# Weights converted with three DVE passes and two ACT passes per pair of pieces, the first block's attention ahead of the conversion, the checks moved behind it

## The chip, the cores and the metric

One core of a Trainium2 chip runs the program. It has five engines with a queue each: PE (TensorE, matrix products), DVE (VectorE), ACT (ScalarE), POOL (GpSimd) and SP (SyncE, which here issues all DMAs). Each queue is worked off in order. [...] The metric is the device time of one execution in microseconds (us).

## The reference

A recurrent attention (RWKV-6) over 4 batches, 8 heads, 768 steps and 48 channels, followed by a two-layer network with a hard-swish between the layers:

```python
for t in range(S):
    kt, vt, rt, wt = (k[:, :, t], v[:, :, t], r[:, :, t], w[:, :, t])
    cur = np.einsum('bhd,bhe->bhde', u[None] * kt, vt)
    y[:, :, t] = np.einsum('bhd,bhde->bhe', rt, state + cur)
    state = wt[:, :, :, None] * state + np.einsum('bhd,bhe->bhde', kt, vt)
...
x = np.ascontiguousarray(attn_out.transpose(0, 2, 1, 3)).reshape(B * S, H * D)
h = x @ w_in
relu6 = np.clip(h + 3.0, 0.0, 6.0)
g = h * relu6 / 6.0
return (g @ w_out).astype(np.float32)
```

x is 3072 x 384, w_in 384 x 2048 and w_out 2048 x 384. [...]

## The kernel before, in words

The 3072 tokens are 24 chunks of 128 (six per batch); three chunks are a block, so there are 8 blocks. For each chunk:

- `load` (L90) issues two DMAs on SP: `feat_in` (r, k, w with the channels on the partitions) and `tok_in` (r, k, v with the tokens there). Three and four buffers.
- `prep` (L138) makes the running product `W` of w (DVE scan, L141), its reciprocal `inv` (DVE, L145), `R` and `K` (POOL, L148 and L149), the tokens' own term `rk` and `dg` (POOL L154 and L155, DVE L157), and spreads `dg` on the diagonal of a tile `A` for all 8 heads (POOL, L160). For the checks it notes the largest w (`w_max`, DVE L150) and the last running product (`w_min`, DVE L152).
- `score` (L165): K times R on PE into `a_ps` (L170), then DVE copies the part above the diagonal into `A` (L173).
- `turn_k` and `write`: PE turns K (L184), ACT copies it (`kn`, L186), PE makes the chunk's state (L195), DVE adds it to `base` (L203, L205), POOL multiplies it with W to the new state `S` (L207).
- `read` (L212): PE adds the part from the state (L223) and the part from `A` (L228); ACT copies the output into `xT` and `x3` (L233, L234). After a block's third chunk six small DMAs on SP move `x3` into `xT` (L239).

For each block the network runs: 16 times `up` (L241: three PE products L246, on ACT `r6` L249, on DVE the gate `g` L251; four PSUM buffers named `mm`), then for each of 3 chunks 4 pieces of `down` (L256: four products L264 each, at the end ACT copies `o`, L268, and SP stores it). A float32 product is two passes on PE, so an `up` is six passes and a whole block of `up` 96, as many as a block of `down`.

The weights come in 32 pieces (16 of w_in, 16 of w_out, 128 x 384 words each) through `weights` (L31): a DMA into `bits` (three buffers, L42), then seven DVE passes (L49 to L58) that take mantissa, exponent and sign apart and put a float32 together. `some_weights` hands out the pieces between the steps of the chunks: 2 before chunk 0, then 3, 2 and 3 in each chunk, so that all are handed out within the first four chunks or so. A list `todo` holds the network's pieces of the finished blocks; each chunk takes a share of it so that PE has work between its own steps.

The code is written in program order; a scheduler and the tile pools decide where an instruction stands on its engine, so the order below is that of the built program. At the end a flag is made of w_max and w_min (L324 to L331). If it were set, `general_path` would compute everything again; with these inputs it is not taken.

Of the kernel before, what the change touches and what calls it, by code (L numbers as in the profile page):

```python
# [18 lines left out]
L = 128  # L19
GP = 64  # L20
LEVELS = 7
BC = 3
LEAST = 2.0 ** -60

# [39 lines left out]
def fast_path(tc, feat, tok, ub, moe_w_in, moe_w_out, out, flag, n_chunks):  # L64
# [15 lines left out]
    with ExitStack() as ctx:  # L80
# [21 lines left out]
        load(1)  # L102

        w_in = const.tile([128, NFC, NCC, 128], F32, name="w_in")
        w_out = const.tile([128, NFC, DM], F32, name="w_out")
        weights = weight_loader(nc, io, wk, w_in, w_out, moe_w_in, moe_w_out)
# [28 lines left out]
        w_max = const.tile([PR, NT], F32, name="w_max")  # L135
        w_min = const.tile([PR, NT, P], F32, name="w_min")

        def prep(i):  # L138
            d = st[i]
            W_ = wk.tile([PR, P * (L + 1)], F32, name="W")  # L140
            nc.vector.tensor_tensor_scan(out=W_, data0=d["w"], data1=restart.rearrange("q p t -> q (p t)"),  # L141
                                         initial=0.0, op0=ALU.mult, op1=ALU.add)
            W = W_.rearrange("q (p t) -> q p t", p=P)
            inv = wk.tile([PR, P, L], F32, name="inv")
            nc.vector.reciprocal(out=inv, in_=W[:, :, 1:])  # L145
# [3 lines left out]
            nc.gpsimd.tensor_mul(K, d["k"], inv)  # L149
            nc.vector.tensor_reduce(out=w_max[:, i:i + 1], in_=d["w"], axis=AX.X, op=ALU.max,  # L150
                                    apply_absolute_value=True)
            nc.vector.tensor_copy(out=w_min[:, i, :], in_=W[:, :, L])  # L152
            rk = wk.tile([L, HD], F32, name="rk")
            nc.gpsimd.tensor_mul(rk, d["rt"], d["kt"])  # L154
            nc.gpsimd.tensor_mul(rk, rk, u_bc)  # L155
            dg = wk.tile([L, H, 1], F32, name="dg")
            nc.vector.tensor_reduce(out=dg.rearrange("s h o -> s (h o)"), in_=rk.rearrange("s (h d) -> s h d", d=D),  # L157
                                    axis=AX.X, op=ALU.add)
            A = wk.tile([L, H, L], F32, name="A")
            nc.gpsimd.tensor_mul(A, ident.rearrange("s (o t) -> s o t", o=1).to_broadcast([L, H, L]),  # L160
                                 dg.to_broadcast([L, H, L]))
            d.update(W=W, R=R, K=K, A=A)
# [79 lines left out]
        def up(bk, f):  # L242
# [7 lines left out]
            g = wk.tile([128, MB], F32, name="g", bufs=NFC + 4)  # L250
# [22 lines left out]
        pieces = [("in", f) for f in range(NFC)] + [("out", f) for f in range(NFC)]  # L273

        def some_weights(n):
            for piece in pieces[:n]:
                weights(*piece)
            del pieces[:n]

        def mlp(n):  # L280
            for _ in range(min(n, len(todo))):
                f, bk, j = todo.pop(0)
                f(bk, j)
# [3 lines left out]
        prep(0)  # L287
        prep(1)
        some_weights(2)
        done = 0  # L290
        for i in range(NT):
            goal = max(0, (i - BC + 1) * per_block // BC - lag) - done
            done += max(goal, 0)
            left = goal
# [7 lines left out]
            if i + 2 < NT:  # L302
                load(i + 2)
            score(i)
            turn_k(i)
            some(1)
            if i + 1 < NT and i > 0:
                prep(i + 1)
            some(2)
            some_weights(3)  # L310
            write(i)
            some(1)
            some_weights(2)
            read(i)
            some(left)
            some_weights(3)
            if i % BC == BC - 1:
                bk = i // BC
                todo.extend([(up, bk, f) for f in range(NFC)] + [(down, bk, c) for c in range(BC * QD)])
                if i == NT - 1:  # L320

                    low = wk.tile([PR, 1], F32, name="low", bufs=1)
                    top = wk.tile([PR, 1], F32, name="top", bufs=1)
                    nc.vector.tensor_reduce(out=low, in_=w_min.rearrange("q i p -> q (i p)"), axis=AX.X, op=ALU.min,  # L324
                                            apply_absolute_value=True)
                    nc.vector.tensor_reduce(out=top, in_=w_max, axis=AX.X, op=ALU.max)
                    nc.vector.tensor_scalar(out=low, in0=low, scalar1=LEAST, scalar2=None, op0=ALU.is_lt)
                    nc.vector.scalar_tensor_tensor(out=top, in0=top, scalar=1.0, in1=low, op0=ALU.is_gt, op1=ALU.max)
                    n_ps = pp.tile([1, 1], F32, name="ps")
                    nc.tensor.matmul(n_ps, lhsT=top, rhs=ones[0:PR, :], start=True, stop=True)  # L330
                    nc.vector.tensor_copy(out=flag, in_=n_ps)  # L331
# [240 lines left out]
def kernel(  # L572
# [3 lines left out]
    tok: bass.AP,  # L576
    ub: bass.AP,
# [19 lines left out]
    fast_path(tc, feat, tok, ub, moe_w_in, moe_w_out, out, flag, n_chunks)  # L597
# [5 lines left out]
_INS = ['feat', 'tok', 'ub', 'ug', 'moe_w_in', 'moe_w_out']  # L603
# [59 lines left out]
```

## Time and profile before

| what | value |
|---|---|
| runs | 720.85, 721.9, 722.49 us, median 721.9 |
| the profiled execution | 722.04 us, span 720.0 us |
| busy in the span | PE 624.5 us (87%), DVE 360.1, POOL 185.7, ACT 128.4 |
| mean granted PE clock | 0.936 of full |
| HBM | 43.49 MB read, 4.72 MB written |

The span goes from the first to the last instruction of the program; the rest of the execution's time lies around it. In the profile a line such as `L49 DVE TENSOR_SCALAR man<-bits ... x32 | 19.4, 606` is a group: line, engine, operation, what it writes from what, shapes, count, then busy us in all and mean ns of one, then the engine's idle time before these and what ended it. PEld is PE's weight load, which runs beside its products.

### The profile page before, as it was taken

The page shows a single profiled execution, that of the slowest core. Times are in us where ns is not written, and L with a number is a line of the kernel's source. Part 1 is how long each engine was busy: PE and PEld are TensorE (multiplying, and loading weights), DVE is VectorE, ACT ScalarE, POOL GpSimd, SP SyncE. Part 2 cuts the span into 40 slices and gives each one's busy share as a digit, 9 for nine tenths or more (in the row PEclk, how much of TensorE's full clock was granted, in tenths as well). Part 3 has the DMA queues.
Part 4 walks back from the last instruction along what each step waited for, and adds up shares of the span by engine and source line. Part 5 has one row for each costly group of instructions (what it writes and reads, how often), then busy time and mean ns, then how long its engine had stood idle before and what let it go on. Part 6 is the DMA issues. An engine that isn't in the chain of part 4 may idle for free.

```text
span 720.0 us, 6998 instructions
## 1 busy us (share of the span) xinstructions
PE 624.5 (87%) x2706; PEld 392.4 (54%) x2706; DVE 360.1 (50%) x548; ACT 128.4 (18%) x269; POOL 185.7 (26%) x148
## 2 busy tenths in 40 slices
PE   1341373779999999999999999999999999999996
PEld 1330251546666666666666666666666666655553
DVE  6999999998136525640346337512463152101200
ACT  0010011112013201320123012210331023102300
POOL 5532252345143223322313413420342020000000
PEclk9975575779999999999999999999999999999999
DMA  8454444423030122211112203120210000000000
GB/s 253 156 166 148 149 148 143 126 72 99 31 93 34 39 90 68 73 64 53 45 50 72 90 16 117 54 71 12 82 34 9 22 12 1 8 24 11 1 12 25
DMA packets 20410, 49.93 MB, mean 69 GB/s; under 512 B 2448, under 2 KB 12560, under 8 KB 20368
## 3 DMA queue, kind: packets, MB, share of 16 engines
q1 hardware_dynamic: 20368, 49.40, 22.2%
q8 instruction: 23, 0.38, 0.2%
q14 instruction: 19, 0.16, 0.1%
HBM read 43.49 MB, written 4.72 MB: 67 GB/s over the span
## 4 chain that ended last, share of the span: by engine, by line
PE 78%; DVE 19%; DMA 2%; POOL 1%; issue 0%; ACT 0%; ACTq 0%; DVEq 0%; POOLq 0%
PE mm L264 35%; PE mm L246 33%; PE a_ps L170 3%; PE ps L228 3%; DVE man L49 2%; DVE inv L145 2%; DVE mag L56 2%; DVE mag L51 2%; PE ps L223 2%; PE ps L195 2%; DVE ex L55 2%; DVE ex L52 1%; DVE W L141 1%; DVE w_out L58 1%; DVE ex L54 1%; PE ps L184 1%
## 5 line engine op out<-in xcount | busy, mean ns | idle before, releaser
L246 PE MATMUL mm<-xT,w_in 128*128 128x384 f32 x768 | 266.9, 504 | 10.4 <-DMA xT<-x 6.6
L264 PE MATMUL mm<-w_out,g 128*128 128x384 f32 x768 | 255.0, 488 | 0.0
L246 PEld LDWEIGHTS mm<-xT,w_in 128*128 128x128 f32 x768 | 148.4, 197 | 110.9 <-issue 16.4
L264 PEld LDWEIGHTS mm<-w_out,g 128*128 128x128 f32 x768 | 143.6, 190 | 96.5 <-issue 2.4
L251 DVE SCALAR_TENSOR_TENSOR g<-r,mm 128x384 f32<-128x384 f32 x128 | 69.5, 550 | 113.0 <-ACT r L249 112.5
L249 ACT ACTIVATE r<-mm,half 128x384 f32<-128x384 f32 x128 | 74.4, 581 | 209.3 <-PE mm L246 178.5
L207 POOL TENSOR_TENSOR S<-base,W 112x448 f32<-112x448 f32 x20 | 19.7, 983 | 254.8 <-DVE base L205 180.1
L145 DVE RECIPROCAL inv<-W 112x512 f32<-112x512 f32 x24 | 80.4, 3349 | 0.6
L160 POOL TENSOR_TENSOR A<-ident,dg 128x1024 f32<-128x1024 f32 x24 | 49.8, 2076 | 41.2 <-PE ps L228 21.2
L170 PE MATMUL a_ps<-R,K 48*128 48x128 f32 x384 | 33.0, 317 | 31.0 <-POOL K L149 31.0
L173 DVE COPY_PREDICATED A<-mask,a_ps 128x1024 f32<-128x1024 uint8 x24 | 31.2, 1301 | 57.0 <-PE a_ps L170 56.9
L170 PEld LDWEIGHTS a_ps<-R,K 48*128 48x128 f32 x384 | 27.7, 216 | 45.2 <-POOL K L149 34.5
L233 ACT COPY xT<-ps 48x384 f32<-48x384 f32 x48 | 22.7, 473 | 155.6 <-PE ps L228 155.2
L148 POOL TENSOR_TENSOR R<-feat_in,W 112x512 f32<-112x512 f32 x24 | 32.3, 1346 | 69.3 <-DVE W L141 66.5
L228 PE MATMUL ps<-A,tok_in 128*48 128x128 f32 x384 | 29.4, 302 | 21.4 <-DVE A L173 21.4
L223 PE MATMUL ps<-R,S 112*112 112x128 f32 x160 | 23.9, 296 | 25.3 <-POOL S L207 25.3
L141 DVE TENSOR_TENSOR_SCAN W<-feat_in,restart 112x516 f32<-112x516 f32 x24 | 34.3, 1430 | 18.9 <-POOL S L207 14.8
L149 POOL TENSOR_TENSOR K<-feat_in,inv 112x512 f32<-112x512 f32 x24 | 30.8, 1282 | 36.3 <-DVE inv L145 13.7
L223 PEld LDWEIGHTS ps<-R,S 112*112 112x112 f32 x160 | 22.3, 195 | 31.1 <-POOL S L207 26.3
L157 DVE TENSOR_REDUCE dg<-rk 128x8 f32<-128x384 f32 x24 | 13.2, 549 | 48.1 <-POOL rk L155 48.1
L228 PEld LDWEIGHTS ps<-A,tok_in 128*48 128x48 f32 x384 | 22.6, 135 | 26.6 <-issue 13.1
L268 ACT COPY o<-mm 128x384 f32<-128x384 f32 x24 | 11.5, 479 | 117.5 <-PE mm L264 108.3
(42 smaller groups left out, 303.2 us busy)
## 6 DMA issues: line engine op xcount, KB each, us to landing
feat_in<-in_feat_dram SPq DMA_DIRECT2D x24, 673.8 KB, 4.9
tok_in<-in_tok_dram SPq DMA_DIRECT2D x24, 576.0 KB, 3.9
bits<-in_moe_w_in_dram SPq DMA_DIRECT2D x16, 384.0 KB, 3.3
bits<-in_moe_w_out_dram SPq DMA_DIRECT2D x16, 384.0 KB, 3.1
out_dram<-o SPq DMA_DIRECT2D x24, 192.0 KB, 1.9
xT<-x SPq DMA_DIRECT2D x48, 24.0 KB, 2.5
u_bc<-in_ub_dram SPq DMA_DIRECT2D x1, 192.0 KB, 7.0
```

The source lines that it names most:

```text
L141: nc.vector.tensor_tensor_scan(out=W_, data0=d["w"], data1=restart.rearrange("q p t -> q (p t)"), initial=0.0, op0=ALU.mult, op1=ALU.add)
L145: nc.vector.reciprocal(out=inv, in_=W[:, :, 1:])
L148: nc.gpsimd.tensor_mul(R, d["r"], W[:, :, :L])
L160: nc.gpsimd.tensor_mul(A, ident.rearrange("s (o t) -> s o t", o=1).to_broadcast([L, H, L]), dg.to_broadcast([L, H, L]))
L170: nc.tensor.matmul(a_ps[:, g, p, :], lhsT=d["K"][rows, p, :], rhs=d["R"][rows, p, :], start=True, stop=True)
L173: nc.vector.copy_predicated(out=d["A"].rearrange("s (p g) t -> s g p t", g=2), mask=mask.rearrange("s (o x t) -> s o x t", o=1, x=1).to_br ...
L223: nc.tensor.matmul(y_ps[:, p, :], lhsT=st[i - 1]["S"][:, p, :], rhs=d["R"][:, p, :], start=(p == 0), stop=False, skip_group_check=True)
L228: nc.tensor.matmul(y_ps[g * GP:g * GP + D, p, :], lhsT=d["v"][:, h, :], rhs=d["A"][:, h, :], start=(first and p == 0), stop=(p == P - 1), ...
L246: nc.tensor.matmul(h_ps, lhsT=w_in[:, f, j, :], rhs=b["xT"][:, j, :], start=(j == 0), stop=(j == NCC - 1))
L249: nc.scalar.activation(out=r6, in_=h_ps, func=ACT.Relu, bias=half, scale=1.0 / 6.0)
L251: nc.vector.scalar_tensor_tensor(out=g, in0=r6, scalar=1.0, in1=h_ps, op0=ALU.min, op1=ALU.mult)
L264: nc.tensor.matmul(o_ps, lhsT=b["g"][f][:, c * L:(c + 1) * L], rhs=w_out[:, f, :], start=(f == 0), stop=(f == NFC - 1))
```

## The change

Six things change in `fast_path`; `general_path` keeps the old conversion.

1. The pieces are converted in 16 pairs (768 words per partition) by `fast_weights`. ACT makes a small integer from each low word in two passes (`more`, L93 and L94), DVE shifts and masks the high word (`top`, L95 and L97) and adds both (L99). This holds for a limited range of exponents.
2. The attention of chunks 0, 1 and 2 stands in the program ahead of all conversion; `load(2)`, `load(3)` and `load(4)` are issued before the first pair's DMAs.
3. The 16 conversions are put in front of the first block's 16 `up` pieces: three pairs before the first, the other 13 spread over the 16.
4. The check of w no longer runs in `prep`: it reads w again from DRAM (`wflat`, 6 pieces of 128 x 1536), and both weight matrices are read again to check the exponents (16 pieces of 128 x 768, two reduces each). Two of these 22 checks follow each chunk from chunk 6 on; they share the buffers of `bits`.
5. The diagonal of `A` is made by ACT, one pass per head (L225), instead of one POOL instruction (L160), and `w_min` is copied by ACT (L216) instead of DVE.
6. `g` has 19 buffers instead of 20.

```diff
+def fast_weights(nc, io, wk, w_in, w_out, moe_w_in, moe_w_out):
...
+        bits = io.tile([128, n], I64, name="bits", bufs=3)
+        for x in range(2):
+            nc.sync.dma_start(out=bits.rearrange("p (c j) -> p c j", j=128)[:, x * m:(x + 1) * m], in_=srcs[x])
...
+        nc.scalar.activation(out=more, in_=lo, func=ACT.Copy, bias=2.0 ** 23, scale=2.0 ** -29)
+        nc.scalar.activation(out=more.bitcast(I32), in_=more, func=ACT.Copy, bias=-2.0 ** 23, scale=1.0)
+        nc.vector.tensor_scalar(out=top, in0=hi, scalar1=3, scalar2=0x3FFFFFF8,
+                                op0=ALU.logical_shift_left, op1=ALU.bitwise_and)
+        nc.vector.scalar_tensor_tensor(out=top, in0=hi, scalar=-0x40000000, in1=top,
+                                       op0=ALU.bitwise_and, op1=ALU.bitwise_or)
+        nc.vector.tensor_tensor(out=dst, in0=top, in1=more.bitcast(I32), op=ALU.add)
...
+        def vet_w(j):
+            t = io.tile([128, VN], F32, name="bits", bufs=3)
+            nc.sync.dma_start(out=t, in_=wflat[:, j * VN:(j + 1) * VN])
+            nc.vector.tensor_reduce(out=w_max[:, j:j + 1], in_=t, axis=AX.X, op=ALU.max, apply_absolute_value=True)
+
+        def vet_weights(which, j):
...
+            nc.sync.dma_start(out=t, in_=src[:, j * n:(j + 1) * n])
+            hi = t.bitcast(F32).rearrange("p (j two) -> p j two", two=2)[:, :, 1]
+            for o, op in ((word_max, ALU.max), (word_min, ALU.min)):
+                nc.vector.tensor_reduce(out=o[:, which, j:j + 1], in_=hi, axis=AX.X, op=op, apply_absolute_value=True)
...
-            nc.vector.tensor_reduce(out=w_max[:, i:i + 1], in_=d["w"], axis=AX.X, op=ALU.max,
-                                    apply_absolute_value=True)
-            nc.vector.tensor_copy(out=w_min[:, i, :], in_=W[:, :, L])
+            nc.scalar.copy(out=w_min[:, i, :], in_=W[:, :, L])
...
-            nc.gpsimd.tensor_mul(A, ident.rearrange("s (o t) -> s o t", o=1).to_broadcast([L, H, L]),
-                                 dg.to_broadcast([L, H, L]))
+            for h in range(H):
+                nc.scalar.activation(out=A[:, h, :], in_=ident, func=ACT.Copy, scale=dg[:, h])
...
+        prep(0)
+        prep(1)
+        attend(0)
+        prep(2)
+        attend(1)
+        attend(2)
+        ahead = 3
+        convs = [(weights, which, f) for which in ("in", "out") for f in range(0, NFC, 2)]
+        first = pieces_of(0)
+        for p in range(NFC):
+
+            upto = ahead + -(-(len(convs) - ahead) * (p + 1) // NFC)
+            before = 0 if p == 0 else ahead + -(-(len(convs) - ahead) * p // NFC)
+            first[p] = convs[before:upto] + first[p]
+        todo.extend(first)
+        load(3)
+        prep(3)
...
+            attend(i, some)
+            if i + 1 < NT:
+                prep(i + 1)
+            some(left)
+            if i >= 2 * BC:
+                for f, *args in vets[:2]:
+                    f(*args)
+                del vets[:2]
```

Here `attend` is `score`, `turn_k`, `write` and `read` of a chunk with shares of `todo` between them.

On DVE, before, right behind the preparation of chunk 1, the first pieces' conversion begins; the predicated copy (L173) of chunk 0 follows it:

```order
L157 TENSOR_REDUCE dg_139<-rk_136 128x8
L49 TENSOR_SCALAR man_145<-bits_143 128x384
L52 TENSOR_SCALAR ex_147<-bits_143 128x384
L51 SCALAR_TENSOR_TENSOR mag_146<-bits_143,man_145 128x384
L54 TENSOR_SCALAR ex_147<-ex_147 128x384
L49 TENSOR_SCALAR man_157<-bits_155 128x384
L55 TENSOR_SCALAR ex_147<-ex_147 128x384
L51 SCALAR_TENSOR_TENSOR mag_158<-bits_155,man_157 128x384
L56 SCALAR_TENSOR_TENSOR mag_146<-mag_146,ex_147 128x384
L52 TENSOR_SCALAR ex_159<-bits_155 128x384
L58 SCALAR_TENSOR_TENSOR w_in_84<-bits_143,mag_146 128x384
```

On DVE, now, the copies L237 of chunks 1 and 2 (A_152, A_216) and their state steps L269 stand ahead of the first pairs (top_368, top_378); `dg_333` to `inv_323` belong to chunk 3:

```order
L237 COPY_PREDICATED A_152<-mask_102,a_ps_225 128x2x4x128
L269 TENSOR_TENSOR base_1_109<-S_185,ps_242 48x4x48 x2
L221 TENSOR_REDUCE dg_333<-rk_330 128x8
L207 SCALAR_TENSOR_TENSOR W_321<-feat_in_317,restart_104 112x516
L211 RECIPROCAL inv_323<-W_321 112x512
L237 COPY_PREDICATED A_216<-mask_102,a_ps_268 128x2x4x128
L269 TENSOR_TENSOR base_0_107<-S_249,ps_285 48x4x48 x2
L95 TENSOR_SCALAR top_368<-bits_365 128x768
L95 TENSOR_SCALAR top_378<-bits_375 128x768
L97 SCALAR_TENSOR_TENSOR top_368<-bits_365,top_368 128x768
L97 SCALAR_TENSOR_TENSOR top_378<-bits_375,top_378 128x768
```

The conversion has moved behind the attention of three chunks and into fewer, longer rows; the adds L99 follow as `ISA w_in_88<-top_368,more_369 128x1536`. A little further, around the first gate (g_411), DVE's order is now:

```order
L207 SCALAR_TENSOR_TENSOR W_495<-feat_in_344,restart_104 112x516
L221 TENSOR_REDUCE dg_507<-rk_504 128x8
L315 SCALAR_TENSOR_TENSOR g_411<-r6_409,mm_405 128x384
L211 RECIPROCAL inv_497<-W_495 112x512
L95 TENSOR_SCALAR top_398<-bits_395 128x768
L95 TENSOR_SCALAR top_416<-bits_413 128x768
```

The gate waits for its `up`, and the reciprocal of chunk 4 and two pairs wait behind it. On SP, before, two pieces of weights go out after the second chunk's loads:

```order
L92 DMA feat_in_80<-in_feat_dram 112x1540
L93 DMA tok_in_81<-in_tok_dram 128x1152
L42 DMA bits_143<-in_moe_w_in_dram 128x3x128
L42 DMA bits_155<-in_moe_w_in_dram 128x3x128
L92 DMA feat_in_167<-in_feat_dram 112x1540
```

On SP, now, the loads of chunks 3 and 4 (feat_in_317 to tok_in_345) stand ahead of the first three pairs, and the six small DMAs of block 0 ahead of the next three:

```order
L132 DMA feat_in_317<-in_feat_dram 112x1540
L133 DMA tok_in_318<-in_tok_dram 128x1152
L132 DMA feat_in_344<-in_feat_dram 112x1540
L133 DMA tok_in_345<-in_tok_dram 128x1152
L86 DMA bits_365<-in_moe_w_in_dram 128x3x128 x2
L86 DMA bits_375<-in_moe_w_in_dram 128x3x128 x2
L86 DMA bits_385<-in_moe_w_in_dram 128x3x128 x2
L132 DMA feat_in_518<-in_feat_dram 112x1540
L303 DMA xT_187<-x3_188 16x384 x6
L86 DMA bits_395<-in_moe_w_in_dram 128x3x128 x2
```

The fifth token buffer in a row (tok_in_345) is the first one's again, so that load waits until chunk 0's output is done, and the first pairs wait behind it.

More of the change, by code (lines that the diff above doesn't have):

```diff
@@ L300, in some @@
                 left -= n
[L302 to L307, printed above, removed]
-                prep(i + 1)
[L309 to L314, printed above, removed]
+            if i + 1 < NT:
+                load(i + 1)
+            attend(i, some)
+            if i + 1 < NT:
+                prep(i + 1)
@@ L315, in fast_path @@
             some(left)
-            some_weights(3)
+            if i >= 2 * BC:
+                for f, *args in vets[:2]:
+                    f(*args)
+                del vets[:2]
             if i % BC == BC - 1:
[L318 to L331, printed above, removed]
@@ L332, in fast_path @@
+        n_ps = pp.tile([1, 1], F32, name="ps")
+        nc.tensor.matmul(n_ps, lhsT=bad, rhs=ones, start=True, stop=True)
+        nc.vector.tensor_copy(out=flag, in_=n_ps)
         mlp(len(todo))
@@ L600 @@
         general_path(tc, feat, tok, ug, moe_w_in, moe_w_out, out, n_chunks)
-_INS = ['feat', 'tok', 'ub', 'ug', 'moe_w_in', 'moe_w_out']
+_INS = ['feat', 'tok', 'wflat', 'ub', 'ug', 'moe_w_in', 'moe_w_out']
 _OUTS = [((3072, 384), 'float32')]
```

88 lines of the change are left out of this document (69 added, 19 removed).

## The prediction

> **What bounds the kernel now.** I read the page's slices first, then the chain that ended last, then the stretch table cut where the chain changes hands.
>
> ```profile
> span 720.0 us, 6998 instructions
> PE   1341373779999999999999999999999999999996
> DVE  6999999998136525640346337512463152101200
> PEclk9975575779999999999999999999999999999999
> PE 78%; DVE 19%; DMA 2%; POOL 1%; issue 0%; ACT 0%; ACTq 0%; DVEq 0%; POOLq 0%
> ```
>
> From the second to the ninth slice (18 us each) DVE is full and PE mostly not, at a lowered granted clock; from the tenth on PE is full. The chain in order of time gives the first pair of passes of a `down` (L264) and the last ones:
>
> ```profile
> 172.34 2.58 PE mm L264 x8
> ...
> 683.54 30.97 PE mm L264 x96
> ```
>
> The last pass ends at 683.54 + 30.97 = 714.51. Cutting there:
>
> ```profile
> 86.97:172.34 85.37, 59.13 (x217) 36.37 (x218) 84.28 (x159) 12.33 (x25) 36.87 (x23) 0.73 0.36 112
> 172.34:714.51 542.17, 542.16 (x2343) 336.62 (x2341) 196.13 (x250) 108.87 (x227) 116.11 (x95) 1.00 0.15 45
> ```
>
> The columns are length, then busy time (count) of PE, PEld, DVE, ACT, POOL, then clock, DMA share and GB/s. After 172.34 PE has 0.01 us of idle time in 542.17, at clock 1.00: that stretch gets shorter only if PE has less to do. From the first `up` (86.97) to the first `down` DVE is busy 84.28 of 85.37 us. So the question of the change is one number: when does the first `down` start?
>
> **What the conversion costs DVE.** By line, shapes apart:
>
> ```profile
> L49 DVE TENSOR_SCALAR man<-bits 128x384 int32<-128x384 int32 x32 | 19.4, 606 | 1.1 <-DMA bits<-in_moe_w_in_dram 1.1
> L51 DVE SCALAR_TENSOR_TENSOR mag<-bits,man 128x384 f32<-128x384 uint32 x32 | 19.1, 597 | 0.0
> L56 DVE SCALAR_TENSOR_TENSOR mag<-mag,ex 128x384 f32<-128x384 f32 x32 | 18.5, 579 | 0.1
> L55 DVE TENSOR_SCALAR ex<-ex 128x384 int32<-128x384 int32 x32 | 14.2, 443 | 0.1
> L52 DVE TENSOR_SCALAR ex<-bits 128x384 int32<-128x384 int32 x32 | 12.8, 398 | 0.0
> L54 DVE TENSOR_SCALAR ex<-ex 128x384 int32<-128x384 int32 x32 | 11.0, 345 | 0.0
> L58 DVE SCALAR_TENSOR_TENSOR w_out<-bits,mag 128x384 int32<-128x384 int32 x16 | 10.9, 679 | 0.0
> L58 DVE SCALAR_TENSOR_TENSOR w_in<-bits,mag 128x384 int32<-128x384 int32 x16 | 9.5, 597 | 0.0
> ```
>
> Together 115.4 us. Undisturbed, one follows the other faster than it lasts:
>
> ```profile
> 29.03 0.35 DVE L52 TENSOR_SCALAR ex<-bits 128x384 int32<-128x384 int32 x1
> 29.30 0.55 DVE L58 SCALAR_TENSOR_TENSOR w_in<-bits,mag 128x384 int32<-128x384 int32 x1
> 29.77 0.35 DVE L54 TENSOR_SCALAR ex<-ex 128x384 int32<-128x384 int32 x1
> ```
>
> From start to start a one-input pass takes 0.27 us and a two-input pass 0.47, so a piece takes 4 x 0.27 + 3 x 0.47 = 2.49 us and a pair 4.98. The durations undisturbed would sum to 32 x (4 x 0.35 + 3 x 0.55) = 97.6; the other 17.8 us are passes held up while POOL works, as here:
>
> ```profile
> 21.85 3.97 DVE L49 TENSOR_SCALAR man<-bits 128x384 int32<-128x384 int32 x1
> 22.75 1.90 POOL L160 TENSOR_TENSOR A<-ident,dg 128x1024 f32<-128x1024 f32 x1
> ```
>
> After, a pair of 768 words is one one-input pass, one two-input pass and the add. Doubling the pitches (an upper bound, since the fixed part is doubled too): 0.54 + 0.94 = 1.48 us. The add (L99) stands in the order as `ISA` on 128x1536, that is on halves of words, and no such instruction is in the trace. Its ends: 0.94 as a two-input pass of 768 words, or 1.88 at one half word in the time of a word. I take 0.94, since L58 writes the same words to the same tile. That makes 2.42 us a pair. [...]
>
> **The start, until the first `up`.** Chunks 0 to 2 now run with no conversion between them. Their chain is read off the trace of before:
>
> ```profile
> 14.72 2.08 PE L170 MATMUL a_ps<-R,K 48*128 48x128 f32 x16 [14.72 <-POOL K L149]
> ...
> 33.34 2.08 PE L170 MATMUL a_ps<-R,K 48*128 48x128 f32 x16
> ...
> 40.57 1.11 PE L228 MATMUL ps<-A,tok_in 128*48 128x128 f32 x16
> ...
> 86.97 1.62 PE L246 MATMUL mm<-xT,w_in 128*128 128x384 f32 x2 [6.64 <-DMA xT<-x]
> ```
>
> ```profile
> 81.41 0.26 ACT L234 COPY x<-ps 48x128 f32<-48x128 f32 x1
> ```
>
> ```profile
> L249 ACT ACTIVATE r<-mm,half 128x384 f32<-128x384 f32 x128 | 74.4, 581 | 209.3 <-PE mm L246 178.5 <-DVE g L251 30.8
> ```
>
> The first scores start at 14.72, and nothing ahead of them gets shorter but small DVE passes. Chunk 1 took 41.68 - 33.34 = 8.34 us from scores to output. Three of those end at 39.7. The diagonal tiles come now from ACT, ahead of `kn` in its queue: eight passes of 128 elements, each between 0.26 (L234, as many elements, no operand per partition) and 0.58 (L249, three times as many, with one), nearer the first; so 2.1 to 4.6 a chunk. Between 0 (hidden behind DVE's reciprocal) and 14 us in all, I take 3. From the last copy to the first `up` went 86.97 - 81.41 = 5.6 us, mostly six small DMAs in line. First `up`: 39.7 + 3 + 5.6 = 48.3. The first three pairs are converted before that: their DMAs stand behind a `tok` load that waits for chunk 0's output (14.72 + 8.34 + 3, about 26), and they have until about 43 to land.
>
> **From the first `up` to the first `down`.** Besides 13 pairs, DVE has 16 gates, 2 reciprocals, a scan, 2 predicated copies and a reduce here:
>
> ```profile
> L145 DVE RECIPROCAL inv<-W 112x512 f32<-112x512 f32 x24 | 80.4, 3349 | 0.6
> L251 DVE SCALAR_TENSOR_TENSOR g<-r,mm 128x384 f32<-128x384 f32 x128 | 69.5, 550 | 113.0 <-ACT r L249 112.5
> L160 POOL TENSOR_TENSOR A<-ident,dg 128x1024 f32<-128x1024 f32 x24 | 49.8, 2076 | 41.2 <-PE ps L228 21.2 <-DVE dg L157 20.1
> L141 DVE TENSOR_TENSOR_SCAN W<-feat_in,restart 112x516 f32<-112x516 f32 x24 | 34.3, 1430 | 18.9 <-POOL S L207 14.8 <-DMA feat_in<-in_feat_dram 3.9
> L173 DVE COPY_PREDICATED A<-mask,a_ps 128x1024 f32<-128x1024 uint8 x24 | 31.2, 1301 | 57.0 <-PE a_ps L170 56.9
> L150 DVE TENSOR_REDUCE w_max<-feat_in 112x1 f32<-112x516 f32 x24 | 16.3, 680 | 18.8 <-DMA feat_in<-in_feat_dram 18.8
> L152 DVE COPY w_min<-W 112x4 f32<-112x4 f32 x24 | 9.5, 395 | 0.0
> L157 DVE TENSOR_REDUCE dg<-rk 128x8 f32<-128x384 f32 x24 | 13.2, 549 | 48.1 <-POOL rk L155 48.1
> ```
>
> 13 x 2.42 + 16 x 0.55 + 2 x 3.35 + 1.43 + 2 x 1.30 + 0.55 = 51.5 us. Three additions. The first gate stands in DVE's order ahead of a reciprocal and conversions and so makes them wait: its `up` is six passes, at the half clock of the row at 86.97 6 x 0.81 = 4.9 us, at full clock 6 x 30.97/96 = 1.9, plus 0.58 for ACT: between 2.5 and 5.5, I take 5. Hold-ups by POOL: between 39 x 17.8/224 = 3 (by instruction) and 17.8 x 13/16 = 14.5 (by pair); POOL loses L160 (2.08 us a chunk), so I take 5. Less 1 for the last add, which no gate waits for. First `down`: 48.3 + 51.5 + 5 + 5 - 1 = 108.8, call it 108.
>
> ACT has 26 conversion passes there, each under 2 x 0.581 = 1.16 us, 30 in all, 16 r6 (9.3) and 16 diagonal passes (4 to 9): at most 49 of 60 us, hidden behind DVE as long as the data is there. DMA:
>
> ```profile
> bits<-in_moe_w_in_dram SPq DMA_DIRECT2D x16, 384.0 KB, 3.3
> feat_in<-in_feat_dram SPq DMA_DIRECT2D x24, 673.8 KB, 4.9
> 54.00:72.00 18.00, 2.31 (x11) 1.72 (x9) 16.92 (x42) 0.53 (x1) 4.33 (x3) 0.50 0.50 148
> SPq L93 <- PE ps L228: 185.0, 18, 18.0
> ```
>
> 13 pairs of 768 KB and about three chunks' loads are 14 MB in 60 us, 233 GB/s; the row had 148 at half the engines' share, so 296 at full share: 47 us, hidden with 13 to spare. SP's token loads wait for PE as before; the bits behind them wait too, but three pairs are in hand.
>
> **After the first `down`** PE's list is the one of before but for eight state passes that move ahead (at most 8 x 0.32 = 2.6 us less, put at zero), so 542.17 us remain. DVE's load there: 196.1, less 18 x (0.68 + 0.40) = 19 for the two steps that leave DVE (L150, L152), plus the checks: 6 reduces of 1536 elements and 32 of 768, from L150's 516 about 2.0 and 1.0 us, 44: about 221 of 542. ACT gains about 45 on 108.9, POOL loses 37. A gate behind a late check may slip: `mm` has four buffers and an `up` takes 1.9 us, so PE feels only more than about 5.8. I put zero on the path. One `g` buffer less costs nothing: the fourth next gate reuses a tile whose last `down` is long past.
>
> **Sum.** 720.0 - (172.34 - 108) = 655.7 us of span. The profiled execution took 722.04 in all, 2.04 outside the span, and the median of the runs is 721.9, so: 658 us.
>
> **The rivals.**
> - *The add runs at one half word a step:* 13 x 0.94 = 12 us more, 670. For it: the 1536 in the order. Against: the bytes are those of 768 words. 0.09.
> - *No cost for ACT's diagonals, full clock and no hold-ups:* 108 - 3 - 2.5 - 5 = 97.5, 647. For it: POOL's work falls. 0.07.
> - *PE's clock, not the conversion, sets the start,* so that the change does not do what it says: 96 `up` passes at half clock are 62 us and three chunks 25, the first `down` at 48 + 87 = 135, 685. For it: clock 0.50 in the row from 54. Against: 0.73 between 86.97 and 172.34, although PE waited for DVE. [...] 0.08.
> - *DMA sets the pace:* if 148 GB/s is all that such loads give, 14 MB take 95 us, first `down` at 143, 693. Decides below 233 GB/s. Against: the share of 0.50. 0.06.
> - *Slower than before: the checks stop PE.* 22 checks stand in DVE's line ahead of gates, their DMAs in SP's line behind loads and outputs that wait. If each held PE for its landing and reduces (3.3 + 2.0), that is 117 us, less the 64 gained: +53, 775. It decides at 64/22 = 2.9 us of idle PE per check. Against: four `mm` buffers, and DVE under half busy. 0.03.
>
> **How the numbers follow.** The forecast (first `down` at 99 to 117) gets 0.67. With 670 and 647 the range 644 to 676 holds 0.83. Faster 0.96, within 0.2% (1.4 us, about what can be told here) 0.01, slower 0.03, all of it the checks.
>
> **What would show it.** Right: a first `up` near 48, the first `down` near 108, then about 542 us of PE without gaps; the add near 0.94; DVE full between the two. Wrong: DVE idle there with waits on bits or on r6, clock 0.5 through it, or idle PE time later that ends on gates behind the checks.

## The result, and the profile after

| | before | after |
|---|---|---|
| median of 4 runs | 722.19 us (720.85 to 722.49) | 648.43 us (647.21 to 649.35) |
| profiled execution | 722.04, span 720.0 | 649.35, span 647.6 |
| first `up` | 86.97 | 47.95 |
| first `down` | 172.34 | 98.57 |
| mean granted PE clock | 0.936 | 0.982 |

The ratio after to before is 0.898, 95% interval 0.896 to 0.900: 73.8 us less. The forecast was 658 (644 to 676). The first `down` is given here as the chain of waits has it; the timeline of single instructions puts it 0.16 us earlier in both (98.41 after), since products overlap (after, the last two passes of `up` start at 97.76 and last 0.81 us, to 98.57), and the experiments' times below are of that kind. Lines have moved in the changed file: `up` is L310, `r6` L313, the gate L315, `down` L328, the scores L234, `kn` L250.

The busy lines and the granted clock of the page, in 40 slices of 16.2 us:

```profile
PE   0688989999999999999999999999999999999996
DVE  4899999789873651145431852134530533002200
PEclk9889969999999999999999999999999999999999
```

PE, which before was full from the tenth slice on, is full from the seventh. The stretch table, cut at the first `up`, the first `down` and the last `down` (length; busy time and count of PE, PEld, DVE, ACT, POOL; clock, DMA share, GB/s):

```profile
0.00:47.95 47.95, 24.48 (x200) 20.99 (x200) 36.60 (x38) 22.55 (x59) 27.71 (x29) 0.89 0.72 205
47.95:98.57 50.62, 43.23 (x175) 26.73 (x174) 50.43 (x58) 35.11 (x65) 17.94 (x12) 0.90 0.86 280
98.57:641.86 543.29, 542.05 (x2334) 335.48 (x2333) 231.81 (x272) 157.48 (x393) 90.08 (x83) 1.00 0.25 79
```

Read against the rows of before: the second stretch shrank from 85.37 to 50.62 us and DVE is still busy for all of it; the last has PE busy 542.05 us where it was 542.16. In this program, too, the time of the first `down` tells nearly the whole result. The three passes of the conversion on DVE, by group:

```profile
L97 DVE SCALAR_TENSOR_TENSOR top<-bits,top 128x768 int32<-128x768 int32 x16 | 15.1, 956 | 0.0
L95 DVE TENSOR_SCALAR top<-bits 128x768 int32<-128x768 int32 x16 | 12.4, 785 | 0.1
L99 DVE CUSTOM_DVE_ANT_0 w_out<-top,more 128x1536 uint16<-128x1536 uint16 x8 | 8.3, 1041 | 0.0
L99 DVE CUSTOM_DVE_ANT_0 w_in<-top,more 128x1536 uint16<-128x1536 uint16 x8 | 8.2, 1050 | 0.0
```

44.0 us together, where the seven passes took 115.4. Undisturbed the add lasts 0.94 us, as it does in this row:

```profile
104.45 0.94 DVE L99 CUSTOM_DVE_ANT_0 w_out<-top,more 128x1536 uint16<-128x1536 uint16 x1
```

### The profile page after: what moved, and what is told of

Same layout as the page of the kernel before. It is cut to its first block, busy times and chain, and to the rows that moved or that the text cites. A ratio compares the mean times of both kernels' runs of the same rounds, so it can differ in the third digit from the quotient of the medians.

```text
span 647.6 us, 7143 instructions
## 1 busy us (share of the span) xinstructions
PE 609.8 (94%) x2706; PEld 383.2 (59%) x2706; DVE 318.8 (49%) x366; ACT 215.6 (33%) x517; POOL 135.7 (21%) x124
## 4 chain that ended last, share of the span: by engine, by line
PE 80%; DVE 9%; DMA 3%; POOL 3%; issue 2%; ACT 1%; SPq 0%; DVEq 0%; POOLq 0%; ACTq 0%
PE mm L328 37%; PE mm L310 32%; PE a_ps L234 3%; PE ps L292 3%; PE ps L287 2%; DVE inv L211 2%; PE ps L259 2%; DMA bits<-in_wflat_dram 1%; PE ps L248 1%; DVE W L207 1%; DVE w_in L99 1%; DVE top L97 1%; DMA bits<-in_moe_w_in_dram 1%; DMA feat_in<-in_feat_dram 1%; POOL K L215 1%
## 5 line engine op out<-in xcount | busy, mean ns | idle before, releaser
L310 PE MATMUL mm<-xT,w_in 128*128 128x384 f32 x768 | 258.3, 492 | 2.8 <-DVE g L315 2.8
L328 PE MATMUL mm<-w_out,g 128*128 128x384 f32 x768 | 255.1, 488 | 0.0
L310 PEld LDWEIGHTS mm<-xT,w_in 128*128 128x128 f32 x768 | 144.0, 191 | 100.8 <-DVE g L315 5.2
L328 PEld LDWEIGHTS mm<-w_out,g 128*128 128x128 f32 x768 | 143.6, 190 | 96.5 <-issue 2.4
L315 DVE SCALAR_TENSOR_TENSOR g<-r,mm 128x384 f32<-128x384 f32 x128 | 69.3, 550 | 114.7 <-ACT r L313 114.4
L313 ACT ACTIVATE r<-mm,half 128x384 f32<-128x384 f32 x128 | 73.7, 579 | 141.3 <-PE mm L310 137.8
L225 ACT ACTIVATE A<-ident,dg 128x128 f32<-128x128 f32 x192 | 60.3, 389 | 7.1 <-DVE dg L221 6.8
L237 DVE COPY_PREDICATED A<-mask,a_ps 128x1024 f32<-128x1024 uint8 x24 | 31.3, 1306 | 47.7 <-PE a_ps L234 47.6
L234 PE MATMUL a_ps<-R,K 48*128 48x128 f32 x384 | 30.4, 298 | 17.8 <-POOL K L215 17.8
L234 PEld LDWEIGHTS a_ps<-R,K 48*128 48x128 f32 x384 | 25.4, 198 | 30.5 <-POOL K L215 18.7
L216 ACT COPY w_min<-W 112x4 f32<-112x4 f32 x24 | 4.7, 197 | 99.0 <-DVE W L207 99.0
L218 POOL TENSOR_TENSOR rk<-tok_in 128x384 f32<-128x384 f32 x24 | 26.3, 1097 | 41.7 <-DMA tok_in<-in_tok_dram 40.7
L250 ACT COPY kn<-ps 128x448 f32<-128x448 f32 x20 | 10.6, 530 | 57.5 <-PE ps L248 57.4
L259 PE MATMUL ps<-tok_in,kn 128*112 128x96 f32 x160 | 21.4, 283 | 7.7 <-ACT kn L250 7.7
```

Of the source, the lines that this page charges most:

```text
L225: nc.scalar.activation(out=A[:, h, :], in_=ident, func=ACT.Copy, scale=dg[:, h])
L234: nc.tensor.matmul(a_ps[:, g, p, :], lhsT=d["K"][rows, p, :], rhs=d["R"][rows, p, :], start=True, stop=True)
L237: nc.vector.copy_predicated(out=d["A"].rearrange("s (p g) t -> s g p t", g=2), mask=mask.rearrange("s (o x t) -> s o x t", o=1, x=1).to_br ...
L259: nc.tensor.matmul(kv_ps[:, p].rearrange("q g e -> q (g e)"), lhsT=d["kn"][:, p, :], rhs=d["v"][:, 2 * p:2 * p + 2, :].rearrange("s h e -> ...
L310: nc.tensor.matmul(h_ps, lhsT=w_in[:, f, j, :], rhs=b["xT"][:, j, :], start=(j == 0), stop=(j == NCC - 1))
L313: nc.scalar.activation(out=r6, in_=h_ps, func=ACT.Relu, bias=half, scale=1.0 / 6.0)
```

## The experiments

Each is the program after with one edit, but for e2, which is the program before with one. The theory: the first `down` sets the time, DVE's list sets the first `down`, and the chunks' chain sets the first `up`. In the rows and the table below the stretch from the last `down` to the end (5.5 to 5.7 us in all of them) is left out.

**e1: the old conversion in the new order.** All else stays as in the program after, the diagonals on ACT and the late checks too. The weights are float64 in the reference and reach the kernel as 64-bit integers; `lo` and `hi` are the two halves of each. The body of the pair's conversion is exchanged for the seven passes, twice per pair:

```diff
-        nc.scalar.activation(out=more, in_=lo, func=ACT.Copy, bias=2.0 ** 23, scale=2.0 ** -29)
...
+        for x in range(2):
+            part = slice(x * n // 2, (x + 1) * n // 2)
+            dst, lo, hi = dsts[:, part], los[:, part], his[:, part]
...
+            nc.vector.tensor_scalar(out=man, in0=hi, scalar1=0xFFFFF, scalar2=0x100000,
+                                    op0=ALU.bitwise_and, op1=ALU.bitwise_or)
```

> The changed kernel with the old seven DVE passes a piece, all else as changed (the diagonal on ACT, the order, the checks). Theory A, that DVE's queue up to the first down sets the time and each part adds up: a pair costs DVE 4.98 us instead of about 2.4, some 14 pairs stand ahead of the first down, so that starts 36 us later, near 134, and the time is 684 us (679 to 690). Theory B, that the gain is the order (attention ahead of the conversion) and the passes are hidden anyway: under 665 us.

**e2: the new conversion in the old order.** The program of before with `fast_weights`, 16 pairs handed out one ahead of chunk 0 and two, one and one in each chunk, instead of two pieces ahead and three, two and three in each. As in the program after, `g` has 19 buffers; the exponents of the weights aren't checked in it.

```diff
+        pieces = [("in", f) for f in range(0, NFC, 2)] + [("out", f) for f in range(0, NFC, 2)]
...
-            some_weights(3)
+            some_weights(2)
```

> The kernel before with only the new conversion in pairs (three DVE and two ACT passes), handed out two pairs, one and one in each chunk after one pair ahead. It leaves out the check of the exponents, which the kernel before has not either. Theory A: DVE, full until 160 us in the kernel before, is rid of about 56 us of queue time, so the first down starts near 116 and the time is 666 us (655 to 676). Theory B, that the order is what counts: 690 us or more.

Measured: e1 688.70 us (ratio to before 0.954, 0.952 to 0.957), e2 675.95 (0.937, 0.934 to 0.939). The stretches from first `up` to first `down` and on to the last, of e1 and then of e2:

```profile
46.13:136.81 90.68, 56.37 (x174) 31.79 (x172) 90.49 (x208) 17.09 (x42) 25.07 (x12) 0.76 0.50 162
136.81:680.86 544.05, 543.63 (x2334) 336.44 (x2334) 238.23 (x295) 155.23 (x389) 90.38 (x83) 1.00 0.25 78
```

```profile
77.34:125.96 48.62, 42.40 (x184) 26.08 (x184) 46.97 (x52) 18.17 (x32) 28.69 (x20) 0.91 0.52 154
125.96:668.28 542.32, 542.32 (x2343) 336.77 (x2341) 195.74 (x251) 108.87 (x227) 116.01 (x95) 1.00 0.15 45
```

In e1 the first `up` comes as early as after (46.13), but DVE is busy for 90.49 of the 90.68 us that follow. In e2 that stretch is as short as after (48.62), but the first `up` stands at 77.34. So the two halves of the change act mostly on different stretches: the order on the first, the passes on the second. Not wholly, for the passes alone bring the first `up` from 86.97 to 77.34 too. Alone the two give 33.5 and 46.2 us; together 73.8, so 5.9 overlap. e1 fell inside what the theory expected, towards the end, e2 at its upper edge; both rivals fell.

**e5, e6: one pass more per pair.** e5 issues the first pass on DVE (L95) twice, e6 the first pass on ACT (L93).

```diff
+        nc.vector.tensor_scalar(out=top, in0=hi, scalar1=3, scalar2=0x3FFFFFF8,
+                                op0=ALU.logical_shift_left, op1=ALU.bitwise_and)
```

```diff
+        nc.scalar.activation(out=more, in_=lo, func=ACT.Copy, bias=2.0 ** 23, scale=2.0 ** -29)
```

> The changed kernel with DVE's first pass of each pair (the shift and mask) done twice, the second time over the first. Theory A, that DVE's queue sets the first down: 0.47 us a pair more, some 14 pairs ahead of the first down, 6.5 us, 655 us (653 to 657). Theory E, that DMA, ACT or PE's clock sets the pace there and DVE has room: 650 us or less.

> The changed kernel with ACT's first pass of each pair done twice, the second time over the first. ACT has 0.84 us a pair more, some 12 us ahead of the first down. Theory A, that DVE sets the pace and ACT has room: 648 to 651 us. Theory E, that ACT's queue is the bound: 657 us or more.

Measured: e5 654.94 us (0.905, 0.903 to 0.908), 6.5 more than after; e6 650.29 (0.898, 0.895 to 0.901), 1.9 more, with an interval that overlaps that of after. Of e5, then e6:

```profile
48.00:103.05 55.05, 45.06 (x174) 26.52 (x172) 54.60 (x71) 35.45 (x66) 16.53 (x12) 0.88 0.78 262
103.05:648.76 545.71, 542.81 (x2334) 335.58 (x2334) 233.90 (x274) 157.13 (x392) 90.43 (x83) 1.00 0.25 78
```

```profile
50.75:100.81 50.06, 43.71 (x174) 26.55 (x173) 48.31 (x57) 42.54 (x76) 16.96 (x12) 0.90 0.87 280
```

With 16 short passes more DVE's stretch grows from 50.46 to 55.05 us, and 2.3 us more pass behind it (545.71 against 641.86 - 98.41 = 543.45). With 16 passes more on ACT, busy 42.54 us there instead of 35.11, the stretch is 50.06, with 1.75 us of idle time on DVE. DVE is the bound between first `up` and first `down`, and ACT's work is hidden behind it. Ahead of the first `up` it is not: in this profile that comes at 50.75 instead of 47.95, the copy `kn` of chunk 3 standing on ACT behind one doubled pass more (45.70 instead of 44.51) and PE's last steps being slower (3.61 us from the product with `S` to the first `up` instead of 1.99).

**e3: the diagonals back on POOL.**

```diff
-            for h in range(H):
-                nc.scalar.activation(out=A[:, h, :], in_=ident, func=ACT.Copy, scale=dg[:, h])
+            nc.gpsimd.tensor_mul(A, ident.rearrange("s (o t) -> s o t", o=1).to_broadcast([L, H, L]),
+                                 dg.to_broadcast([L, H, L]))
```

> The changed kernel with the diagonal of A made by POOL again (one instruction a chunk). Theory A: about 6 chunks' 2.08 us on POOL hold DVE up by 2 to 5 us, and ACT comes to kn earlier, for which PE waited 7.7 us in the changed kernel: the two about cancel, 644 to 652 us. Theory C, that the relief of POOL and so of DVE's hold-ups is a main part of the gain: 656 us or more.

Measured: 654.34 us (0.906, 0.904 to 0.908), between the two theories, and both had the place wrong. The stretches (its profiled execution, 657.13 us, is the slowest of its four, so they overstate the cost somewhat):

```profile
0.00:54.94 54.94, 28.52 (x200) 24.08 (x200) 41.15 (x41) 13.05 (x27) 36.81 (x34) 0.88 0.66 194
54.94:106.88 51.94, 45.17 (x174) 27.71 (x173) 49.35 (x57) 30.29 (x49) 20.22 (x14) 0.87 0.84 268
```

The second stretch is 1.5 us longer, the first 7.0. DVE's scans and PE's timeline tell why; of e3:

```profile
27.02 1.90 POOL L224 TENSOR_TENSOR A<-ident,dg 128x1024 f32<-128x1024 f32 x1
```

```profile
27.10 2.91 DVE L207 TENSOR_TENSOR_SCAN W<-feat_in,restart 112x516 f32<-112x516 f32 x1 [0.35 <-POOL S L271]
```

```profile
30.84 1.81 PE L259 MATMUL ps<-tok_in,kn 128*112 128x96 f32 x8 [2.95 <-ACT kn L250]
```

The same scan after:

```profile
24.60 1.23 DVE L207 TENSOR_TENSOR_SCAN W<-feat_in,restart 112x516 f32<-112x516 f32 x1 [0.34 <-POOL S L271]
```

Two diagonals stand in POOL's line ahead of the state `S` of chunk 0, so chunk 2's scan starts 2.5 us later, and it lasts 2.91 us instead of 1.23 while POOL makes a third. On ACT the copy `w_min` waits for that scan, `kn` of chunk 1 stands behind it, and PE's state product waits for `kn`. Chunk 3's scan (at 36.38) lasts 2.91 us too, again beside a diagonal. The edit costs 5.9 us in the medians, because POOL is on the chain of the chunks before the first `up`.

**e4: no checks.** The 22 checks, with their loads, are left out; the flag is made of constants.

```diff
-        vets = [(vet_w, j) for j in range(n_w)]
-        if f64:
-            vets += [(vet_weights, which, j) for which in range(2) for j in range(n_v)]
+        vets = []
```

> The changed kernel without the 22 checks behind chunk 6 (their loads and reduces are left out; w_max and the two word tables are filled with constants). Theory A: PE's two gaps after the first down (0.99 and 0.25 us) go, 646.5 to 648 us. Theory D, that the checks cost more than the gaps show, through DMA or queues: 644 us or less.

Measured: 646.29 us (0.895, 0.893 to 0.897), 2.1 less than after, against a limit of 1.9 that was expected.

```profile
97.25:638.69 541.44, 541.44 (x2335) 336.06 (x2333) 195.50 (x231) 158.44 (x393) 90.33 (x83) 1.00 0.16 48
```

PE has no idle time left in that stretch (1.24 us after), and its products there take 0.8 us less (541.44 instead of 542.21). In this profile the first `down` comes 1.2 us earlier too, with the first `up`, which no check can touch; so the checks' own price is between 1.2 and 2.1 us.

**e7: three `mm` buffers instead of four.**

```diff
-            h_ps = pp.tile([128, MB], F32, name="mm", bufs=4)
+            h_ps = pp.tile([128, MB], F32, name="mm", bufs=3)
```

> The changed kernel with three PSUM buffers for the up and down products instead of four. Theory F, that the first down came earlier than forecast because four buffers let PE finish the last ups ahead of DVE's last gates: the first down moves 1 to 5 us later. If the lead plays no part, the first down stays within 1 us of 98.5. What three buffers cost after the first down is not part of either and is read apart.

Measured: 655.11 us (0.906, 0.902 to 0.910).

```profile
48.01:103.40 55.39, 46.14 (x190) 27.90 (x188) 53.39 (x62) 37.01 (x69) 18.05 (x12) 0.87 0.81 268
103.40:649.02 545.62, 541.92 (x2318) 335.13 (x2318) 229.22 (x267) 154.97 (x389) 90.09 (x83) 1.00 0.24 77
```

The first `down` is 5.0 us later, at the upper end of what was expected, with the first `up` in place. `up`s and `down`s use the same `mm` buffers. With four of them the first `down` gets the one that the thirteenth of the 16 gates gives back, with three that of the fourteenth, and here it waits for it:

```profile
103.40 7.04 PE L328 MATMUL mm<-w_out,g 128*128 128x384 f32 x21 [0.53 <-DVE g L315]
```

DVE has 3.86 us of gates and conversions left behind the first `down` (to 107.26), where it had 6.75 (98.57 to 105.32). That is 2.9 of the 5.0 us. The rest is that DVE's own list ends 1.9 us later, with 2.0 us of idle time in the stretch (55.39 - 53.39). In the last stretch PE's idle time triples, from 1.24 to 3.70 us.

**e8, e9, e10, e11, e12: what still binds.** e8 puts all of the first block's `up`s and conversions ahead of chunk 3's attention:

```diff
-        done = 0
+        mlp(NFC)
+        done = NFC
+        early = {BC: 2, BC + 1: 3, BC + 2: 2}
...
-            left = max(0, (i - BC + 1) * per_block // BC - lag - done)
+            left = early.get(i, max(0, (i - BC + 1) * per_block // BC - lag - done))
```

> The changed kernel with all 16 ups of block 0 ahead of the attention of chunks 3 to 5 in the program, and two, three and two downs handed out in these chunks. Theory A, that the first down comes when DVE has done what stands ahead of it: two chunks' scan, reciprocal, reduce and predicated copy (some 12 us) go behind it, so the first down starts near 87, and the time is 638 to 646 us if PE finds no gaps later. Theory G, that this work is given back later, since PE then waits for the attention of chunks 3 to 5: 647 us or more, with gaps of as much after the first down.

e9 makes the diagonal in `attend`, behind `turn_k`, so that `kn` can go first on ACT:

```diff
+        def diagonal(i):
+            A = wk.tile([L, H, L], F32, name="A")
+            for h in range(H):
+                nc.scalar.activation(out=A[:, h, :], in_=ident, func=ACT.Copy, scale=st[i]["dg"][:, h])
...
+            turn_k(i)
+            diagonal(i)
```

> The diagonal of A is made in the attention, behind the scores and behind the copy of kn, so that PE's state product need not wait for eight passes of ACT per chunk. In the run after, PE waited 7.7 us for kn in all, part of it ahead of the first up (47.95). Theory H (the start is a chain through ACT, and the diagonal's place in ACT's queue is part of it): the first up comes 1 to 4 us earlier, the first down as much earlier, since DVE is full between them: 644 to 647.5 us. Rival I (the chain until the first up runs through reciprocal, POOL's products and the predicated copy, and ACT's order is free): first up within 0.7 us of 47.95, and 647.5 to 649.5 us. Or a third way: the predicated copy, which needs the diagonal, now ends later, and the first up with it, by up to 2.5 us a chunk: 649 to 654.

e10 is e8 with chunk 4's load and preparation ahead of the last four `up`s; e11 is e10 with the edit of e9; e12 is e8 with the edit of e9.

```diff
+        mlp(NFC - 4)
+        prep(BC + 1)
+        mlp(4)
```

> As e8_ups_first (all of the first block's ups and conversions ahead of chunk 3's attention, 643.0 us), with chunk 4's preparation put ahead of the last four ups, so that its K is ready when PE comes to it. Theory G (the one PE gap of 3.34 us there and the half clock behind it cost some 3.3 to 6 us): the gap goes, and the first down comes later by what DVE is given ahead of it (a scan and a reciprocal, 1.4 + 3.4, and a small reduce, of which the ups already in PSUM hide a part): 637 to 641 us. Rival: the DVE work only changes its place, the first down slips by the same 4 to 5 us as the gap was wide, or the gap opens at another chunk: 642 to 645.

> Both of the edits before together. If they act apart, its difference to the run after is the sum of the two, since one lies ahead of the first up and the other behind the first down: by theories H and G 634 to 639 us; by their rivals 642 to 649.

> e8_ups_first (the first block's ups and conversions together, 643.0 us) with the diagonal of A behind the copy of kn, as in e9_kn_first, where the first up came 2.4 us earlier and the time fell by 1.4. Theory H: the start is shortened here too and nothing behind it changes, so the first up comes at 45 to 46.5, the first down at 79 to 80.5, and the time is 640.5 to 642.5 us. Rival, from e11_both (where the two together gave nothing more than the one): PE's first waits behind the first down grow by what the start gives, and the time stays at 642.5 to 645 us.

| | median, us | ratio to before | first `up` | first `down` | to the last `down` | PE idle there |
|---|---|---|---|---|---|---|
| after | 648.43 | 0.896 to 0.900 | 47.95 | 98.41 | 543.45 | 1.24 |
| e8 | 643.04 | 0.887 to 0.891 | 47.57 | 81.37 | 554.95 | 3.35 |
| e9 | 647.03 | 0.894 to 0.898 | 45.55 | 95.82 | 543.27 | 1.06 |
| e10 | 646.59 | 0.893 to 0.897 | 46.63 | 84.22 | 557.63 | 4.91 |
| e11 | 646.55 | 0.893 to 0.897 | 45.78 | 84.48 | 555.19 | 5.61 |
| e12 | 638.68 | 0.883 to 0.889 | 45.52 | 77.81 | 553.21 | 2.22 |

e8 takes DVE's work for chunks 4 and 5 out of the stretch. The time is inside what theory A expected (638 to 646). The first `down` comes 17.0 us earlier (87 had been expected, it was 81.37), PE has the chunks' steps to do afterwards (551.60 us of products instead of 542.21), and one wait opens, for the K of chunk 4:

```profile
96.93 2.08 PE L234 MATMUL a_ps<-R,K 48*128 48x128 f32 x16 [3.34 <-POOL K L215]
```

e10 was to close it. It did, but the time came out above the theory (637 to 641) and above its rival too (642 to 645). In kind the rival was right: the first `down` slips by 2.9 us against e8, and other gaps open. PE now waits for the masked `A` of chunk 3, which on DVE comes behind the conversion's last passes (row below), and 2.4 us more of idle time follow at three later places; why was not followed further.

```profile
94.68 1.24 PE L292 MATMUL ps<-A,tok_in 128*48 128x128 f32 x16 [2.49 <-DVE A L237]
```

e9 brings the first `up` 2.4 us earlier, as theory H had it. The three programs with this edit have it at 45.5 to 45.8; after, e7, e8 and e10, whose edits lie behind it, have it at 46.6 to 48.0. The median of e9 is 1.4 us lower, but the intervals overlap, so that gain is not shown. On top of e10 the edit gave nothing (e11, 646.55 where the two theories had 634 to 639). On top of e8 the median fell again (e12):

```profile
45.52:77.81 32.29, 32.29 (x101) 18.95 (x101) 32.15 (x47) 26.25 (x38) 2.38 (x2) 0.98 0.93 317
77.81:631.02 553.21, 550.99 (x2429) 343.72 (x2427) 246.27 (x284) 165.99 (x420) 106.49 (x95) 1.00 0.27 86
```

From the first `up` on PE has 2.22 us of idle time. e12, at 0.886 of before, is faster than both kernels. Its 638.68 lies below theory H's 640.5 to 642.5, as its first `down` (77.81) lies ahead of the 79 to 80.5 expected. Its interval (0.883 to 0.889) overlaps that of e8, so that the second edit helps there is likely and not shown.

## Why the prediction was right

**The mechanism** held. The sum came to a span of 655.7 us and the profile shows 647.56, 8.1 less: 9.4 from the first `down` (98.57, not 108), given back 1.1 between first and last `down` and 0.2 at the end. The time around the span was 1.8 instead of 2.04, and the median lies 0.9 below the profiled execution.

**The start** (48.3) was right within 0.4, and in part by luck. The scores began at 15.52, 0.8 late, and PE's timeline has the ends of the three chunks:

```profile
15.52 2.08 PE L234 MATMUL a_ps<-R,K 48*128 48x128 f32 x16 [15.52 <-POOL K L215]
...
29.01 1.81 PE L259 MATMUL ps<-tok_in,kn 128*112 128x96 f32 x8 [3.35 <-ACT kn L250]
...
41.20 1.08 PE L292 MATMUL ps<-A,tok_in 128*48 128x128 f32 x16
...
47.95 2.52 PE L310 MATMUL mm<-xT,w_in 128*128 128x384 f32 x7
```

The third output ends at 42.28 (42.7 by the sum), so the three chunks took 26.8 us where 28.0 had been put. The 3 us for ACT's diagonals were well sized: the chain that ended last goes through them twice, for 3.5 us in all.

```profile
26.06 2.35 ACT A L225 x8
...
35.97 1.18 ACT A L225 x4
```

The first `up` starts 5.67 us after the third output (5.6 by the sum), but what fills this time is not what was forecast. In the kernel before PE waited there for the small DMAs. Here PE has no idle time right before 47.95: from 42.21 on it works at chunk 3's scores and output, with one wait of 1.19 us for `kn`. The fourth small DMA, the last one that the first product needs, started at 44.95 and had landed by 46.9. That term had the right size for another reason.

The eight passes of a chunk:

```profile
17.05 2.45 ACT L225 ACTIVATE A<-ident,dg 128x128 f32<-128x128 f32 x8 [3.35 <-DVE dg L221]
19.40 0.51 ACT L250 COPY kn<-ps 128x448 f32<-128x448 f32 x1
```

2.45 us, near the low end of the 2.1 to 4.6. What the prediction did not see is the other side of the exchange: the same diagonals on POOL would have cost the start up to 7.0 us (e3, by its profile).

**The step that was off is the stretch from first `up` to first `down`**: 60.5 us by the sum (to 108.8, before it was called 108), 50.62 by the trace. Two of its terms were mis-sized.

- *"Less 1 for the last add, which no gate waits for."* Not one add lies behind the first `down`, but three gates and the passes of the last pairs:

```profile
94.79 0.54 DVE L315 SCALAR_TENSOR_TENSOR g<-r,mm 128x384 f32<-128x384 f32 x1
...
100.86 0.54 DVE L315 SCALAR_TENSOR_TENSOR g<-r,mm 128x384 f32<-128x384 f32 x1
...
102.66 0.53 DVE L315 SCALAR_TENSOR_TENSOR g<-r,mm 128x384 f32<-128x384 f32 x1
...
103.99 0.53 DVE L315 SCALAR_TENSOR_TENSOR g<-r,mm 128x384 f32<-128x384 f32 x1
```

From 98.57 to the end of this work at 105.32 are 6.75 us. Four `mm` buffers hold `up`s that wait for their gates, and the first `down` needs only the first gates and pieces and one free buffer, which the thirteenth gate (94.79) gives it. e7, with one buffer less, leaves 2.9 us less behind it and bears this out. The term was 5.75 too small.

- *The first gate's wait, 5 us.* The gate stands at 52.26, 4.3 us after the first `up`, so its own delay was sized well. But the conversion of the third pair, a scan and the small reduce lie ahead of it in DVE's order, and DVE is idle for 50.62 - 50.43 = 0.19 us in the whole stretch. The wait was covered by other work: 4.8 too much.

Together these are 10.55 us, 0.7 more than the 9.9 by which the stretch was too long. That the other terms fit so well is luck, for two errors among them nearly cancel. The sum has one scan and one small reduce, while the trace has two of each in the stretch, three state steps (L269) and the rest of the third pair: some 5.5 us more, by the rows' durations. On the other side, a pair undisturbed goes by in 2.21 us from start to start (0.47 + 0.87 + 0.87, from 92.98 on), not 2.42, and a gate in 0.47, not 0.55: some 4 us less for 13 pairs and 16 gates.

The hold-ups by POOL were right in size: the sixteen conversions would take 16 x (0.55 + 0.95 + 0.94) = 39.0 us undisturbed and took 44.0, 5 us, most of it in this stretch, such as here, where POOL's product `rk` runs. That POOL is the cause is read from such pairs of rows, here (1.75 us instead of 0.94) and in e3, where a scan takes 2.91 us instead of 1.23 with POOL's diagonal beside it.

```profile
88.64 1.75 DVE L99 CUSTOM_DVE_ANT_0 w_out<-top,more 128x1536 uint16<-128x1536 uint16 x1
```

```profile
88.39 1.19 POOL L219 TENSOR_TENSOR rk<-rk,u_bc 128x384 f32<-128x384 f32 x1
```

DVE's list is not the whole of the stretch, and the sum has no term for its end. The chain that ended last leaves DVE with chunk 5's reciprocal at 84.4 us and goes through K on POOL to PE, which from 85.76 on has no idle time before the first `down`:

```profile
84.44 1.28 POOL K L215
85.76 1.64 PE a_ps L234 x10
87.40 4.14 PE mm L310 x6
91.54 1.03 PE a_ps L234 x6
92.57 6.00 PE mm L310 x18
```

The two run close together: the fourteenth `up`, the first of the last 18 passes, needed the buffer that the tenth gate gave back at 91.73.

**The rival of 647** came nearer to the measured time (648.43) than the forecast did, and not by its reasons. It had no cost for ACT's diagonals, full clock and no hold-ups. The trace has 3.5 us of diagonals on the chain, the clock at 0.90 between first `up` and first `down`, and 5 us of hold-ups.

**The add** is at the low end, 0.94 us for 768 words (1536 halves), as long as the two-input pass L97 on the same words (0.94 at 93.92). The rival of 670 falls.

**DMA** gave 280 GB/s at a share of 0.86, above the 233 needed, so the rival of 693 falls; e1 at 0.50 and 162 shows that the low share of before was a matter of demand. **The clock** was 0.90 in the stretch, and PE was busy 43.23 of 50.62 us: the rival of 685 falls, although PE ran at half the clock from 85.76 to 92.31.

**The checks** were put at zero on the path and cost 1.2 to 2.1 us. Their reduces were sized well (1.73 us for 1536 elements against 2.0, 0.94 for 768 against 1.0), and the four buffers hide nearly all of them. PE's waits for a gate:

```profile
PE mm L310 <- DVE g L315: 2.8, 3, 1.5
```

Of these three waits two, of 0.99 and 0.25 us, lie behind the first `down` (they begin at 162.13 and 166.95), among the checks, and e4 has neither. The rival of 775, which needed more than 2.9 us per check, falls: 2.1 us over 22 checks are 0.1 each.

## What to carry to other kernels

When one engine is full from a point on to the end, the question of any change ahead of that point is when it starts; find the one instruction that marks it and add up what stands ahead of it on the engine that feeds it. What the feeding engine still has to do *behind* the mark must be counted too, and the depth of the buffers between the two tells how much that is. A step taken from one engine's line and given to another's is priced on both: the line it leaves may be on the chain of the start, and in the line it joins it can be moved behind what somebody waits for.

## What the runs showed of the hardware

**In the trace of after the granted clock changed on a grid of 3.41 us.** Up to the first `down` it was 0.50 from 27.45 to 34.28, from 37.70 to 41.11 and from 82.07 to 92.31, two, one and three steps of that length, with 12 between 41.11 and 82.07. Cut at these steps, the slow stretch between first `up` and first `down` reads:

```profile
78.65:82.07 3.42, 0.88 (x3) 0.19 (x1) 3.42 (x3) 1.67 (x5) 3.34 (x3) 1.00 0.79 248
82.07:85.48 3.41, 2.05 (x8) 1.73 (x8) 3.41 (x3) 1.51 (x4) 2.06 (x2) 0.50 1.02 341
85.48:88.90 3.42, 3.14 (x13) 2.31 (x14) 3.42 (x5) 2.24 (x8) 2.38 (x3) 0.50 0.72 199
88.90:92.31 3.41, 3.41 (x11) 1.73 (x9) 3.41 (x4) 1.85 (x3) 0.68 (x1) 0.50 0.75 253
92.31:95.72 3.41, 3.41 (x12) 2.07 (x12) 3.41 (x7) 1.36 (x3) 0.00 (x0) 1.00 0.72 240
```

A step in which PE was busy for 0.88 of 3.42 us was followed by half the clock; one with 3.14 of 3.42 at half the clock was followed by another at half, one that was full by the full clock. Earlier in this trace one with 3.35 of 3.41 (37.70 to 41.11) was followed by the full clock as well. The busy time of a step alone does not tell whether the clock falls: one with 1.77 us (34.28 to 37.70) was followed by half the clock, one with 1.73 (54.76 to 58.18) was not.

**The passes of the diagonal on ACT** (L225, 128 elements with an operand per partition) took 389 ns each in the mean of the 192. Eight of them took 2.45 us in the row at 17.05, so by an estimate from these two numbers they started every 0.29 us, (2.45 - 0.39) / 7, and each overlapped the one before by some 0.1 us.
